# Sparse attention with a gated feed-forward network: chunks of 512 local tokens, one last chunk for the global tokens of all batches, gate buffers by row pairs

## The chip, the cores and the metric

The kernel runs on one core of one Trainium2 chip. The metric is the device time of one execution in microseconds (us), as the median of several runs. Lower is better. The engines are TensorE (PE in the profile; PEld is its weight load), VectorE (DVE), ScalarE (ACT), GpSimd (POOL) and SyncE (SP), which issues the transfers (DMA).

## What is computed

Eight batches, eight heads, 512 local and 32 global tokens, head dimension 64. Global queries attend to everything; a local query attends to all global keys and to local keys at most 32 positions away. The result of all heads (544 tokens x 512) goes through a network with 1024 hidden columns, a convolution over three neighbouring tokens and a gate.

```python
s_g  = scale * q_g @ concat(k_g, k_l).T          # 32 global queries, 544 keys
out_g = softmax(s_g) @ concat(v_g, v_l)
s_l  = scale * q_l @ concat(k_g, where(|i-j|<=32, k_l, -1e9)).T
out_l = softmax(s_l) @ concat(v_g, v_l)
x = concat(out_g, out_l)                         # 8 x 544 x 512, global tokens first
h = maximum(x @ w_in, 0)                         # 512 -> 1024
c = sum over k in 0..2 of conv_w[k] * h[token + k - 1]
return (h * sigmoid(c)) @ w_out                  # 1024 -> 512
```

The attention's inputs are float32, the network's weights float64.

## The kernel before, in words

**Attention.** Heads are worked in pairs (n even). Local queries stand in 16 blocks of 32; with the blocks in four groups c of four, `SC` (L291) makes the scores of a pair with 32 small matmuls per head against windows of 128 keys (three local blocks and the global one). `MA` (L319) adds the mask and takes the maximum on DVE, `EX` (L329) is the exponential on ACT, `NS` and `NP` divide by the sum, `DT` (L350) transposes 32 x 32 blocks on DVE into a buffer `pt`, and `PV` (L360) multiplies with the values. `XH` and `XL` (L380) split the result into two float32r parts, high and low, in the tiles `xh` and `xl`, each 128 x 544 for 128 of the 512 columns. The global queries go through `G`, `GM`, `GE`, `GN`, `GT`, `GC`, `GP`, `GO`, `GQ`; `GX` writes their 32 tokens into the first columns of the same tiles.

**Keys.** The keys of a pair come with its queries in one load (`LQ`): 512 query columns and 4 x 7 blocks of 32 keys, where each group c has its own seven blocks, neighbours doubled.

**Network.** It works in units of half a batch (`HALF` = 272 tokens; 16 halves `hh`). `Z` (L475) makes one block of 128 hidden columns of a half with 12 matmuls of 274 columns: four 128-row parts of x, and for each high x high, high x low and low x high. `RE` (L484) is max(0, .)/2 on ACT into `hb`; `C1` (L276, POOL) and twice `C2` (L499, DVE) are the convolution in `t`; for two blocks together `TH` (L508) is the tanh on ACT, `GG` (L513) the gate on DVE, `GH` (L241) and `GL` (L244) its split into the gate tiles `g0` (high) and `g1` (low). These hold all eight blocks of a half, two halves at a time. `O` (L538) makes 128 output columns of a half with 24 matmuls of 272 columns in two parts (`Oa`, `Ob`), `OE` (L241) copies it out of PSUM and `ST` (L550) stores it. Every matmul of `Z` and `O` has weights of its own, so it comes with a weight load.

**Weights.** The float64 weights come in eight chunks (`WD`) into the buffers that later hold the gates, and are turned into a high and a low float32r part: `WA`, `WC`, `WL` (L115 to L215) on ACT and DVE, `WS` (L224 to L226: 512-column matmuls, first float32, then two in float32r) and `WX`.

**Order.** The order on each engine is not written out by hand: `plan` lists all operations with costs, buffers and positions (`POS`, `POS0`), `arranged` runs them through a list of ready operations, and `emit` fixes that order on each engine. Buffers are counted in `SLOTS`; at most two `Z` and two `O` results are in PSUM (`LIMIT`).

```python
SLOTS = dict(
    ps=4, pa=2, x=6, hb=2, qk=5, vf=5, qg=2, p=4, pt=4, r=3, pg=2, pgt=2, og=1, t=2, o=2, wt=2, g0=2, g1=2,
)
LIMIT = dict(h=2, o=2)
```

Of the kernel before, what the change touches and what calls it, by code (L numbers as in the profile page):

```python
# [56 lines left out]
def attn_moe(ctx: ExitStack, tc: tile.TileContext, qk_d, vw_d, qg_d, w_in_d, w_out_d, cw_d, out_d):  # L57
# [9 lines left out]
    gp = ctx.enter_context(tc.tile_pool(name="gp", bufs=2))  # L67
# [106 lines left out]
    def WD(i):  # L174

        t = gp.tile([P, 1024, wpe], WT, name="raw", tag=f"g{i % 2}", padded_shape=[P, NFT * HALF // wpe, wpe])
# [58 lines left out]
    hb = [const.tile([P, 2, HW + 1], F32, name=f"hb{i}") for i in range(SLOTS["hb"])]  # L235
    for t in hb:
        for o in (0, HW):
            nc.vector.memset(t[:, :, o : o + 1], 0.0)
# [41 lines left out]
    def SC(n):  # L280

        qk = heads[n]["qk"]
        for j in range(2):
            heads.setdefault(n + j, {})["s"] = four[SIDE["S", n]][:, j, :].rearrange("p (r x) -> p r x", r=NR)
        for r in range(NR):
            for c in range(4):
                i = NR * c + r
                a = SL + (NK * c + r) * SG
                for j in range(2):
                    rows = slice(j * D, (j + 1) * D)  # L290
                    nc.tensor.matmul(  # L291
                        heads[n + j]["s"][c * SG : (c + 1) * SG, r, :], lhsT=qk[rows, i * SG : (i + 1) * SG],
                        rhs=qk[rows, a : a + P], start=True, stop=True,
                    )

    def G(n):
# [5 lines left out]
        for i in range(3):  # L302
            for c in range(4):
                k = heads[first + 2 * c]["qk"][:, SL:]
                for j in range(2):
                    rows = slice(j * D, (j + 1) * D)
                    if i < 2:
                        kj = k[rows].rearrange("p (c m x) -> p m c x", c=4, m=NK)[:, SLOT[2 * i] : SLOT[2 * i] + 2]
# [142 lines left out]
    def GX(n):  # L451
        pt = gos[n // H][1]
        for ct in range(NCT):
            xh, xl = x_of(n // H, ct)
            cp("GX", xh[:, 0:SG], pt[:, ct * SG : (ct + 1) * SG])
            nc.vector.tensor_tensor(
                out=xl[:, 0:SG], in0=pt[:, ct * SG : (ct + 1) * SG], in1=f(xh)[:, 0:SG], op=ALU.subtract
            )
# [4 lines left out]
    def half_of(hh):  # L463
        return (hh + TURN) % 2

    def Z(u):
        hh, ft = divmod(u, NFT)
        b, half = hh // 2, half_of(hh)
        st = hid[u] = {"h": hb[u // 2 % SLOTS["hb"]][:, u % 2, half : half + HW]}
        ps = st["z"] = bank([P, HW], "ps_h")  # L470
        i = 0
        for ct in range(NCT):
            xh, xl = [x[:, half * (S - HW) : half * (S - HW) + HW] for x in x_of(b, ct)]
            for w, x in ((w_in[0], xh), (w_in[0], xl), (w_in[1], xh)):
                nc.tensor.matmul(ps, lhsT=w[:, ft, ct, :], rhs=x, start=i == 0, stop=i == 3 * NCT - 1)  # L475
                i += 1

    def RE(u):

        half = half_of(u // NFT)  # L480
        o = hid[u]["h"][:, 1 - half : HW - half]
        z = hid[u]["z"][:, half : HW - 1 + half]
# [21 lines left out]


    def TH(u):
        t = hid[u]["two"]
        nc.scalar.activation(out=t, in_=t, func=AF.Tanh)  # L508

    def GG(u):  # L510
        t, half = hid[u]["two"], half_of(u // NFT)
        h = hb[u // 2 % SLOTS["hb"]][:, :, half + 1 : half + 1 + HALF]
        nc.vector.scalar_tensor_tensor(out=t, in0=t, scalar=1.0, in1=h, op0=ALU.add, op1=ALU.mult)  # L513

    def GH(u):
        hh, ft = divmod(u, NFT)
        if hh not in gs:
            gs[hh] = [gp.tile([P, NFT, HALF], F32R, name=f"g{i}") for i in range(2)]
        cp("GH", gs[hh][0][:, ft - 1 : ft + 1, :], hid[u]["two"])

    def GL(u):
        hh, ft = divmod(u, NFT)
        gh, gl = gs[hh]
        sub("GL", gl[:, ft - 1 : ft + 1, :], hid[u]["two"], f(gh)[:, ft - 1 : ft + 1, :])


# [3 lines left out]
    def O(o, part):  # L530
        hh, mt = divmod(o, NCT)
        gh, gl = gs[hh]
        if part == 0:
            ops[o] = bank([P, HALF], "ps_o")
        ps = ops[o]
        for ft in range(part * 4, part * 4 + 4):
            for i, (w, g) in enumerate(((w_out[0], gh), (w_out[1], gh), (w_out[0], gl))):
                nc.tensor.matmul(  # L538
                    ps, lhsT=w[:, mt, ft, :], rhs=g[:, ft, :], start=ft + i == 0, stop=ft == NFT - 1 and i == 2
                )  # L540

    def OE(o):
        hh, mt = divmod(o, NCT)
        t = outs[o] = moe.tile([P, HALF], F32, name="o", bufs=SLOTS["o"])
        cp("OE", t, ops[o])

    def ST(o):
        hh, mt = divmod(o, NCT)
        b, half = hh // 2, half_of(hh)
        nc.sync.dma_start(out=out_d[b, mt, :, half * HALF : (half + 1) * HALF], in_=outs[o])  # L550

    emit(tc, B, dict(
        LQ=LQ, LV=LV, LG=LG, G=G, S=SC, M=MA, E=EX, NS=NS, NP=NP, DT=DT, P=PV,
        XH0=lambda n: XH(n, 0), XH1=lambda n: XH(n, 1), XL0=lambda n: XL(n, 0), XL1=lambda n: XL(n, 1),
        GM=GM, GE=GE, GN=GN, GT=GT, GC=GC, GP=GP, GO=GO, GQ=GQ, GX=GX,
        PZ=Z, RE=RE, C1=C1, Ca=lambda u: C2(u, 0), Cb=lambda u: C2(u, 2), TH=TH, GG=GG, GH=GH, GL=GL,
        Oa=lambda o: O(o, 0), Ob=lambda o: O(o, 1), OE=OE, ST=ST, WD=WD, WA=WA, WC=WC, WH=WH, WL=WL, WS=WS, WX=WX,
# [5 lines left out]
    ps=4, pa=2, x=6, hb=2, qk=5, vf=5, qg=2, p=4, pt=4, r=3, pg=2, pgt=2, og=1, t=2, o=2, wt=2, g0=2, g1=2,  # L563
# [396 lines left out]
```

## Time and profile before

| | us |
|---|---|
| median of 3 runs (573.83 to 576.04) | 574.9 |
| the profiled execution, whole | 573.74 |
| its span, first to last instruction | 572.0 |
| PE busy | 546.3 (96%) |
| PEld busy | 511.7 (89%) |
| DVE busy | 431.0 (75%) |
| ACT busy | 355.1 (62%) |
| POOL busy | 97.3 (17%) |
| DMA: 57.09 MB, mean 100 GB/s | queue with the data busy 27.5% of 16 engines |

The chain that ended last lies on PE for 87% of the span: 34% on `O` (L538), 34% on `Z` (L475), 7% on `PV` (L360), 5% on `SC` (L291). PE's busy time is a sum of pipelined matmuls, whose recorded durations overlap; the pace of a matmul is read from the distance of one start to the next.

### The profile page before, as it was taken

What the parts mean: (1) busy time and instruction counts of PE and PEld (TensorE: products, weight loads), DVE (VectorE), ACT (ScalarE), POOL (GpSimd) and SP (SyncE); (2) the same over time, 40 slices, a digit from 0 to 9 for tenths busy, and PEclk for the clock granted to TensorE, in tenths of its full rate; (3) what the DMA queues carried; (4) which work ended last, traced back from release to release, by engine and by line L of the source; (5) the groups of instructions that cost most, each with busy time, mean ns of one, the idle gap of its engine ahead of it and who ended that gap; (6) DMA issues with size and microseconds to landing.
All of it is one profiled execution on the core that took longest, in us unless ns stands there. A gap on an engine that the chain in (4) does not pass through costs nothing.

```text
span 572.0 us, 23262 instructions
## 1 busy us (share of the span) xinstructions
PE 546.3 (96%) x9904; PEld 511.7 (89%) x9904; DVE 431.0 (75%) x1403; ACT 355.1 (62%) x1140; POOL 97.3 (17%) x171
## 2 busy tenths in 40 slices
PE   4289999999999999999999999999999999999997
PEld 3257888899999999999999999999999999999997
DVE  4999999776889788778967778688676776646561
ACT  5658789685995686649672698279633493313330
POOL 4311142320111110201110111101111021101110
PEclk9589999999999999999999999999999999999999
DMA  8666743015403603043300603050000300000001
GB/s 350 280 241 207 245 158 109 12 29 196 168 15 135 229 21 123 21 158 113 113 31 24 241 13 131 13 193 14 30 30 32 111 13 21 32 22 21 21 31 49
DMA packets 20984, 57.09 MB, mean 100 GB/s; under 512 B 2448, under 2 KB 11664, under 8 KB 19856
## 3 DMA queue, kind: packets, MB, share of 16 engines
q1 hardware_dynamic: 20880, 55.61, 27.5%
q8 instruction: 77, 1.26, 0.9%
q14 instruction: 27, 0.22, 0.1%
HBM read 46.69 MB, written 8.91 MB: 97 GB/s over the span
## 4 chain that ended last, share of the span: by engine, by line
PE 87%; DVE 8%; DMA 2%; issue 1%; ACT 1%; SPq 0%; DVEq 0%; ACTq 0%
PE ps_o L538 34%; PE ps_h L475 34%; PE four L360 7%; PE four L291 5%; DMA raw<-w_in 2%; PE four L428 2%; PE four L312 2%; PE four L412 1%; PE psw L224 1%; DVE pr L319 1%; DVE t L499 1%; DVE pt L350 1%; DVE xl L380 1%; DVE wt L126 1%; PE four L446 1%
## 5 line engine op out<-in xcount | busy, mean ns | idle before, releaser
L475 PE MATMUL ps_h<-xh,w_in 128*128 128x274 f32 x1024 | 222.6, 296 | 0.3 <-issue 0.3
L538 PE MATMUL ps_o<-g,w_out 128*128 128x272 f32 x1536 | 210.8, 290 | 0.0
L538 PEld LDWEIGHTS ps_o<-g,w_out 128*128 128x128 f32 x1536 | 199.1, 188 | 1.1 <-issue 0.4
L475 PEld LDWEIGHTS ps_h<-xh,w_in 128*128 128x128 f32 x1024 | 169.3, 188 | 6.6 <-issue 3.8
L499 DVE SCALAR_TENSOR_TENSOR t<-hb,cw,t 128x272 f32<-128x272 f32 x256 | 125.2, 509 | 32.1 <-POOL t L276 31.1
L475 PE MATMUL ps_h<-xl,w_in 128*128 128x274 f32 x512 | 148.4, 290 | 0.0
L276 POOL TENSOR_SCALAR t<-hb,cw 128x272 f32<-128x272 f32 x128 | 74.0, 584 | 395.4 <-ACT hb L484 247.8
L329 ACT ACTIVATE pr<-pr,negm 128x128 f32<-128x128 f32 x256 | 99.2, 392 | 28.0 <-DVE negm L319 28.0
L475 PEld LDWEIGHTS ps_h<-xl,w_in 128*128 128x128 f32 x512 | 97.0, 189 | 0.2
L484 ACT ACTIVATE hb<-ps_h 128x273 f32<-128x273 f32 x128 | 50.5, 395 | 60.6 <-PE ps_h L475 60.1
L343 ACT ACTIVATE pr<-pr,sums 128x128 f32<-128x128 f32 x224 | 70.4, 394 | 4.7 <-DVE sums L337 4.7
L508 ACT ACTIVATE t<-t 128x544 f32<-128x544 f32 x64 | 42.0, 657 | 44.4 <-DVE t L499 43.9
L360 PEld LDWEIGHTS four<-pt,vf 32*64 32x64 f32 x3584 | 48.7, 133 | 19.2 <-DVE negm L319 12.0
L319 DVE CUSTOM_DVE_ANT_0 pr<-four,mask 128x128 f32<-128x128 f32 x256 | 57.3, 285 | 11.4 <-PE four L291 11.2
L360 PE MATMUL four<-pt,vf 32*64 32x96 f32 (+3 forms) x3584 | 53.1, 246 | 12.8 <-DVE negm L319 11.1
L513 DVE SCALAR_TENSOR_TENSOR t<-t,hb 128x544 f32<-128x544 f32 x64 | 46.0, 720 | 17.8 <-ACT t L508 17.7
L241 ACT CAST g<-t 128x544 fp32r<-128x544 f32 x64 | 40.8, 644 | 20.7 <-DVE t L513 18.1
L241 DVE COPY o<-ps_o 128x272 f32<-128x272 f32 x64 | 28.1, 440 | 33.5 <-PE ps_o L538 33.3
L350 DVE STREAM_TRANSPOSE pt<-pr 128x512 f32<-128x512 f32 x64 | 44.4, 700 | 8.4 <-PE four L360 4.6
L329 ACT ACTIVATION_READ_ACCUMULATOR pr<-pr,negm 128x1 f32 x256 | 48.8, 191 | 0.0
L291 PE MATMUL four<-qk 64*32 64x128 f32 x2048 | 39.1, 282 | 8.9 <-DMA qk<-qk 4.8
L244 DVE TENSOR_TENSOR g<-t,g 128x544 fp32r<-128x544 f32 x56 | 40.3, 722 | 6.0 <-ACT g L241 5.5
(79 smaller groups left out, 393.6 us busy)
## 6 DMA issues: line engine op xcount, KB each, us to landing
qk<-qk SPq DMA_DIRECT2D x32, 704.0 KB, 5.7
vf<-vw SPq DMA_DIRECT2D x32, 448.0 KB, 5.6
out<-o SPq DMA_DIRECT2D x64, 136.0 KB, 1.8
raw<-w_in SPq DMA_DIRECT2D x4, 1024.0 KB, 12.4
raw<-w_out SPq DMA_DIRECT2D x4, 1024.0 KB, 5.0
qgf<-qg SPq DMA_DIRECT2D x8, 64.0 KB, 4.7
cwr<-cw SPq DMA_DIRECT2D x1, 24.0 KB, 10.8
```

The source lines that it names most:

```text
L241: nc.scalar.copy(out=out, in_=in_) if choice(key) == "a" else eng(key).tensor_copy(out=out, in_=in_)
L276: nc.gpsimd.tensor_scalar(out=out, in0=in_, scalar1=by, scalar2=0.0, op0=ALU.mult, op1=ALU.add)
L291: nc.tensor.matmul(heads[n + j]["s"][c * SG : (c + 1) * SG, r, :], lhsT=qk[rows, i * SG : (i + 1) * SG], rhs=qk[rows, a : a + P], start=Tr ...
L319: nc.vector.tensor_tensor_reduce(out=pr[:, r, :], in0=st["s"][:, r, :], in1=mask[:, r].rearrange("p a c -> p (a c)"), op0=ALU.add, op1=ALU ...
L329: nc.scalar.activation(out=st["p"][:, r, :], in_=st["p"][:, r, :], func=AF.Exp, scale=-1.0, bias=st["m"][:, r : r + 1], accum_out=two["r"] ...
L343: nc.scalar.activation(out=p[:, r, :], in_=p[:, r, :], func=AF.Copy, scale=by[:, r : r + 1])
L350: nc.vector.transpose(out=st["pt"].rearrange("p a q -> p (a q)"), in_=st["p"].rearrange("p r x -> p (r x)"))
L360: nc.tensor.matmul(four[c // 2][j * D : (j + 1) * D, c % 2, r0 * SG : (r1 + 1) * SG], lhsT=heads[n]["vf"][rows, j, m, :], rhs=heads[n + j] ...
L475: nc.tensor.matmul(ps, lhsT=w[:, ft, ct, :], rhs=x, start=i == 0, stop=i == 3 * NCT - 1)
L484: nc.scalar.activation(out=o, in_=z, func=AF.Relu, scale=0.5)
L499: nc.vector.scalar_tensor_tensor(out=st["t"], in0=st["h"][:, k : k + HALF], scalar=cw[:, 3 * ft + k : 3 * ft + k + 1], in1=st["t"], op0=AL ...
L538: nc.tensor.matmul(ps, lhsT=w[:, mt, ft, :], rhs=g[:, ft, :], start=ft + i == 0, stop=ft == NFT - 1 and i == 2)
```

## The change

1. **Chunks of the network.** A chunk is now the 512 local tokens of a batch (`Z` and `O` with 512 columns), and one last chunk holds the 32 global tokens of all eight batches: `Z` with 8 x 34 = 272 columns (a batch's globals and its first two local tokens, as neighbours for the convolution), the convolution and `O` with 8 x 35 - 2 = 278 columns, with one zero column between batches. A new tile `xg` keeps the x of these tokens until then: `GX` writes it with two instructions instead of eight, and a new step `XC` on POOL copies two local columns per 128 rows of x. The output is laid out as chunks and put in order outside.
2. **Parts.** `Z` is in two parts: `Za` needs the first two 128-row parts of x, `Zb` the other two. `O` is in four, `Oa` to `Od`, each needing one pair of gate blocks.
3. **Gate buffers by row pairs.** One tile `g` holds high and low part of two blocks (2 x 2 x 512); there are five of them, instead of two sets of eight blocks of 272. The weight chunks use the same five. The weight decoding's buffer `wt` is gone: it shares the two buffers `t` of the convolution.
4. **Transposes in place.** `DT` writes over its source; the buffers are `p` = 6 instead of `p` = 4 and `pt` = 4.
5. **Keys in 22 blocks.** The groups share their neighbours: 22 blocks of 32 keys instead of 28. Queries and keys are loaded apart (`LQ` 256 KB, three buffers; `LK` 352 KB, five buffers) instead of in one load of 704 KB.
6. **Plan.** All positions are new, and the costs follow the new sizes.

```diff
-ROW = (-1, 0, 1, None, 2, 3, 4)
-NK = len(ROW)
-KSEQ = 4 * NK * SG
-SLOT = tuple(ROW.index(x) for x in (0, 1, 2, 3, None))
+ROW = (-1, 0, 1) + sum(((None,) + tuple(range(4 * c + 2, 4 * c + 6)) for c in range(4)), ())[:-1]
+KSEQ = len(ROW) * SG
+NK = 7
+SLOT = (1, 2, 4, 5, 3)
...
-            wf[i] = load.tile([P, 1024], U32, name="wt", bufs=SLOTS["wt"])
+            wf[i] = moe.tile([P, 1024], U32, name="wt", tag="t", bufs=SLOTS["t"])
...
+    xg = const.tile([P, 2, NCT, B, GW], F32R, name="xg")
...
-        st["pt"] = att.tile([P, 4 * NR, SG], F32, name="pt", bufs=SLOTS["pt"])
-        nc.vector.transpose(out=st["pt"].rearrange("p a q -> p (a q)"), in_=st["p"].rearrange("p r x -> p (r x)"))
+        flat = st["p"].rearrange("p r x -> p (r x)")
+        nc.vector.transpose(out=flat, in_=flat)
+        st["pt"] = flat.rearrange("p (a q) -> p a q", q=SG)
...
+    def XC(n):
+        b, h = divmod(n, H)
+        cp("XC", xg[:, :, h // 2, b, SG:GW], f(x_of(b, h // 2))[:, :, 0:2])
...
+        hi, lo = [xg[:, i, :, b, 0:SG] for i in range(2)]
+        cp("GX", hi, pt)
+        nc.vector.tensor_tensor(out=lo, in0=pt, in1=f(hi), op=ALU.subtract)
...
+    def Z(u, part):
+        b, ft = divmod(u, NFT)
+        n = B * GW if last(u) else SL
+        if part == 0:
+            hid[u] = {"z": bank([P, 512], "ps_h")[:, 0:n]}
+        for ct in range(2 * part, 2 * part + 2):
+            xh, xl = [xg[:, i, ct].rearrange("p b x -> p (b x)") if last(u) else x_of(b, ct)[:, i] for i in range(2)]
+            for i, (w, x) in enumerate(((w_in[0], xh), (w_in[0], xl), (w_in[1], xh))):
+                nc.tensor.matmul(
+                    hid[u]["z"], lhsT=w[:, ft, ct, :], rhs=x, start=ct + i == 0, stop=ct == NCT - 1 and i == 2
+                )
...
-            gs[hh] = [gp.tile([P, NFT, HALF], F32R, name=f"g{i}") for i in range(2)]
-        cp("GH", gs[hh][0][:, ft - 1 : ft + 1, :], hid[u]["two"])
+        g = gs[u // 2] = gp.tile([P, 2, 2, SL], F32R, name="g", tag="g")[:, :, :, 0 : width(u)]
+        cp("GH", g[:, 0], mid_of(u))
...
-    ps=4, pa=2, x=6, hb=2, qk=5, vf=5, qg=2, p=4, pt=4, r=3, pg=2, pgt=2, og=1, t=2, o=2, wt=2, g0=2, g1=2,
+    ps=4, pa=2, x=6, hb=2, q=3, k=5, vf=5, qg=2, p=6, r=3, pg=2, pgt=2, og=1, t=2, o=2, g=5,
...
+        if local:
+            ready = [[("XL%d" % k, 8 * b + 2 * ct) for ct in cts for k in range(2)] for cts in ((0, 1), (2, 3))]
+        else:
+            ready = [[("GX", 8 * i + 7) for i in range(b)] + [("XC", 2 * i) for i in range(4 * b)], []]
...
+        for i, key in enumerate(("Oa", "Ob", "Oc", "Od")):
+            before = [("GL", NFT * b + 2 * i + 1)] + ([weight(4 + mt)] if i == 0 else [("O" + "abc"[i - 1], o)])
+            at_o(key, before, [("ps", f"o{o}"), ("o_", f"o{o}o")] * (i == 0), [f"g{4 * b + i}"] + [f"o{o}"] * (i > 0))
```

## Rows read from the trace of the kernel before

**Rows 1.** Busy time by stretch: bounds, length, PE, PEld, DVE, ACT, POOL, clock, DMA.
```profile
0.00:46.20 46.20, 25.96 (x793) 18.17 (x793) 36.97 (x127) 28.04 (x89) 12.25 (x35) 0.82 0.77 292
46.20:72.00 25.80, 25.49 (x371) 21.31 (x371) 25.18 (x73) 22.00 (x57) 4.53 (x6) 1.00 0.65 218
72.00:143.00 71.00, 69.62 (x1382) 62.48 (x1381) 59.31 (x210) 53.03 (x179) 18.44 (x22) 1.00 0.29 99
143.00:500.50 357.50, 357.06 (x6662) 342.33 (x6661) 274.82 (x922) 234.37 (x783) 53.16 (x93) 1.00 0.23 81
500.50:572.00 71.50, 68.20 (x704) 67.37 (x703) 34.67 (x75) 17.62 (x35) 8.87 (x16) 0.99 0.09 29
```

**Rows 2.** PE's longest waits between 0 and 72 us: sum, times, longest.
```profile
PE four L360 <- DVE negm L319: 10.5, 2, 6.6
PE four L291 <- DMA qk<-qk: 4.8, 1, 4.8
PE four L360 <- DVE xl L380: 1.7, 1, 1.7
```

**Rows 3.** The chain that ended last: start, length, engine, line, matmuls.
```profile
46.20 1.72 PE ps_h L475 x12
...
314.70 1.71 PE ps_h L475 x12
...
488.64 1.52 PE ps_h L475 x12
...
553.64 15.15 PE ps_o L538 x120
```

**Rows 4.** PE in order of time at one weight chunk: start, recorded length, operation.
```profile
98.46 1.02 PE L224 MATMUL psw<-wt,ident 128*128 128x512 f32 x2
...
99.55 0.39 PE L226 MATMUL psw<-w_out,minus 128*128 128x512 f32 x1
99.78 1.02 PE L224 MATMUL psw<-wt,ident 128*128 128x512 f32 x2
...
100.86 0.40 PE L226 MATMUL psw<-w_out,minus 128*128 128x512 f32 x1
101.10 0.29 PE L475 MATMUL ps_h<-xh,w_in 128*128 128x274 f32 x1
```

**Rows 5.** The weight loads (PEld) at the same place.
```profile
100.64 0.19 PEld L226 LDWEIGHTS psw<-w_out,minus 128*128 128x128 f32 x1 [0.24 <-issue]
100.87 0.19 PEld L475 LDWEIGHTS ps_h<-xh,w_in 128*128 128x128 f32 x1
```

**Rows 6.** Groups by line and shape: busy us, mean ns, idle before and its releaser.
```profile
L276 POOL TENSOR_SCALAR t<-hb,cw 128x272 f32<-128x272 f32 x128 | 74.0, 584 | 395.4 <-ACT hb L484 247.8 <-DVE g L244 107.9 <-DVE gsum L403 15.4
L244 DVE TENSOR_TENSOR g<-t,g 128x544 fp32r<-128x544 f32 x56 | 40.3, 722 | 6.0 <-ACT g L241 5.5
L380 DVE TENSOR_TENSOR xl<-four,xh 128x256 fp32r<-128x256 f32 x64 | 24.2, 411 | 5.9 <-ACT xh L241 5.5
L126 DVE SCALAR_TENSOR_TENSOR wt<-raw,wt 128x1024 uint32<-128x1024 uint32 x8 | 9.8, 1226 | 0.3
L241 ACT CAST w_in<-wt 128x1024 fp32r<-128x1024 f32 x4 | 4.2, 1052 | 1.7 <-DVE wt L126 1.7
L96 POOL COPY place<-ident 32x32 f32<-32x32 f32 x4 | 0.8, 203 | 0.2
```

**Rows 7.** DVE in order of time: four convolution steps back to back.
```profile
82.00 1.74 DVE L499 SCALAR_TENSOR_TENSOR t<-hb,cw,t 128x272 f32<-128x272 f32 x4
```

**Rows 8.** First and last step of one weight chunk, DVE and PE in order of time.
```profile
48.83 0.69 DVE L122 TENSOR_SCALAR wt<-wt 128x1024 f32<-128x1024 f32 x1
...
58.67 0.40 PE L226 MATMUL psw<-w_out,minus 128*128 128x512 f32 x1
```

**Rows 9.** SP's waits for `SC` to free a query and key buffer: sum, times, longest.
```profile
SPq L259 <- PE four L291: 51.3, 11, 13.0
```

**Rows 10.** The last copy out of PSUM, DVE in order of time.
```profile
568.81 0.44 DVE L241 COPY o<-ps_o 128x272 f32<-128x272 f32 x1 [1.07 <-PE ps_o L538]
```

More of the change, by code (lines that the diff above doesn't have):

```diff
@@ L174, in WD @@
     def WD(i):
-        t = gp.tile([P, 1024, wpe], WT, name="raw", tag=f"g{i % 2}", padded_shape=[P, NFT * HALF // wpe, wpe])
+        t = gp.tile([P, 1024, wpe], WT, name="raw", tag="g", padded_shape=[P, 2048 // wpe, wpe])
         nc.sync.dma_start(out=t.rearrange("p n w -> p (n w)"), in_=w_in_d[:, i] if i < 4 else w_out_d[:, i - 4])
@@ L232, in WX @@
                 cp("WX", lo[:, 512 * k : 512 * k + 512], ps)
-    hb = [const.tile([P, 2, HW + 1], F32, name=f"hb{i}") for i in range(SLOTS["hb"])]
+    xg = const.tile([P, 2, NCT, B, GW], F32R, name="xg")
+    hb = [const.tile([P, 2, SL + 2], F32, name=f"hb{i}") for i in range(SLOTS["hb"])]
     for t in hb:
-        for o in (0, HW):
+        for o in (0, SL + 1):
             nc.vector.memset(t[:, :, o : o + 1], 0.0)
@@ L280, in SC @@
     def SC(n):
-        qk = heads[n]["qk"]
+        q, keys = heads[n]["q"], heads[n]["k"]
         for j in range(2):
@@ L291, in SC @@
                     nc.tensor.matmul(
-                        heads[n + j]["s"][c * SG : (c + 1) * SG, r, :], lhsT=qk[rows, i * SG : (i + 1) * SG],
-                        rhs=qk[rows, a : a + P], start=True, stop=True,
+                        heads[n + j]["s"][c * SG : (c + 1) * SG, r, :], lhsT=q[rows, i * SG : (i + 1) * SG],
+                        rhs=keys[rows, a : a + P], start=True, stop=True,
                     )
@@ L303, in G @@
             for c in range(4):
-                k = heads[first + 2 * c]["qk"][:, SL:]
+                k = heads[first + 2 * c]["k"]
                 for j in range(2):
@@ L451, in GX @@
     def GX(n):
[L452 to L458, printed above, removed]
+        b = n // H
+        pt = gos[b][1].rearrange("p (c x) -> p c x", c=NCT)
+        hi, lo = [xg[:, i, :, b, 0:SG] for i in range(2)]
+        cp("GX", hi, pt)
@@ L460, in attn_moe @@
+        nc.vector.tensor_tensor(out=lo, in0=pt, in1=f(hi), op=ALU.subtract)
     hid = {}
     gs = {}
[L463 to L476, printed above, removed]
@@ L478, in RE, with last, width, rows_of @@
-    def RE(u):
-        half = half_of(u // NFT)
-        o = hid[u]["h"][:, 1 - half : HW - half]
-        z = hid[u]["z"][:, half : HW - 1 + half]
+    def last(u):
+        return u // NFT == B
+    def width(u):
+        return B * GV - 2 if last(u) else SL
+    def rows_of(u, k):
+        return hb[u // 2 % SLOTS["hb"]][:, :, k : k + width(u)]
+    def mid_of(u):
+        return hid[u]["two"][:, :, 0 : width(u)]
+    def Z(u, part):
[9 more added lines that the diff above has]
+                )
@@ L483, in RE @@
+    def RE(u):
+        t, z = hb[u // 2 % SLOTS["hb"]], hid[u]["z"]
+        o = t[:, u % 2, 1 : SL + 1]
+        if last(u):
+            both = t[:, :, 0 : B * GV].rearrange("p a (b x) -> p a b x", b=B)
+            if u % 2 == 0 and u // 2 % (NFT // 2) < SLOTS["hb"]:
+                nc.gpsimd.memset(both[:, :, :, 0:1], 0.0)
+            o, z = both[:, u % 2, :, 1:], z.rearrange("p (b x) -> p b x", b=B)
         if choice("RE") == "a":
@@ L506, in TH @@
     def TH(u):
-        t = hid[u]["two"]
+        t = mid_of(u)
         nc.scalar.activation(out=t, in_=t, func=AF.Tanh)
     def GG(u):
-        t, half = hid[u]["two"], half_of(u // NFT)
-        h = hb[u // 2 % SLOTS["hb"]][:, :, half + 1 : half + 1 + HALF]
-        nc.vector.scalar_tensor_tensor(out=t, in0=t, scalar=1.0, in1=h, op0=ALU.add, op1=ALU.mult)
+        t = mid_of(u)
+        nc.vector.scalar_tensor_tensor(out=t, in0=t, scalar=1.0, in1=rows_of(u, 1), op0=ALU.add, op1=ALU.mult)
     def GH(u):
-        hh, ft = divmod(u, NFT)
@@ L528, in attn_moe @@
+        sub("GL", g[:, 1], mid_of(u), f(g)[:, 0])
     ops, outs = {}, {}
     def O(o, part):
-        hh, mt = divmod(o, NCT)
-        gh, gl = gs[hh]
+        b, mt = divmod(o, NCT)
         if part == 0:
-            ops[o] = bank([P, HALF], "ps_o")
+            ops[o] = bank([P, 512], "ps_o")[:, 0 : width(NFT * b)]
         ps = ops[o]
-        for ft in range(part * 4, part * 4 + 4):
-            for i, (w, g) in enumerate(((w_out[0], gh), (w_out[1], gh), (w_out[0], gl))):
+        g = gs[NFT // 2 * b + part]
@@ L538, in O @@
+        for ft in range(2 * part, 2 * part + 2):
+            for i, (w, k) in enumerate(((0, 0), (1, 0), (0, 1))):
                 nc.tensor.matmul(
-                    ps, lhsT=w[:, mt, ft, :], rhs=g[:, ft, :], start=ft + i == 0, stop=ft == NFT - 1 and i == 2
+                    ps, lhsT=w_out[w][:, mt, ft, :], rhs=g[:, k, ft % 2, :], start=ft + i == 0,
+                    stop=ft == NFT - 1 and i == 2,
                 )
     def OE(o):
-        hh, mt = divmod(o, NCT)
-        t = outs[o] = moe.tile([P, HALF], F32, name="o", bufs=SLOTS["o"])
+        t = outs[o] = moe.tile([P, SL], F32, name="o", bufs=SLOTS["o"])[:, 0 : width(NFT * (o // NCT))]
@@ L592, with cost @@
+    GC=7.81, GP=73.94, GO=69.07, GQ=95.45, GX=31.75, Za=-51.42, Zb=23.49, RE=18.93, C1=19.9, Ca=-110.94,
+    Cb=-28.3, TH=-19.96, GG=-107.88, GH=46.26, GL=17.73, Oa=137.35, Ob=-36.69, Oc=38.34, Od=-17.69, OE=-37.34,
+    ST=-9.22, WD=260.68, WA=43.56, WC=557.46, WH=-14.87, WL=27.97, WS=29.44, WX=-19.5,
+)
+LATE = (277.56, 46.45, 51.62)
+WPOS = [-181.22, -223.58, 13.77, -1.77, 112.11, 84.41, 21.24, -26.67]
 LAST_BATCH = 7
-TURN = 1
-def cost(key, e):
+def cost(key, e, wide=True):
     def act(n, calls=1, src=190, more=0):
@@ L634, in cost @@
     if key in DIFFERENCES:
-        return two(DIFFERENCES[key]) if e == "v" else pool2(DIFFERENCES[key])
+        return two(2 * n) if e == "v" else pool2(2 * n)
     if key == "C1":
-        return act(HALF, more=93) if e == "a" else fast(HALF) if e == "v" else pool1(HALF)
+        return act(n, more=93) if e == "a" else fast(n) if e == "v" else pool1(n + 90)
     if key == "NP":
@@ L682, in op @@
         at[key, i] = len(ops)
-        occ, lat = cost(key, c)
+        wide = key not in UNITS or i < UNITS[key] * B
+        occ, lat = cost(key, c, wide)
         more = int(occ * STRETCH["shared" if e == DVE and key in SHARED else e])
@@ L725, in plan @@
             before = [("DT", e), ("DT", n), ("LV", e)] + [("P", e - 2)] * (e > 0)
-            at_n("P", before, [("pa", x) for x in oo] + [("x", x)], [f"pt{e}", f"pt{n}", f"vf{p}"], i=e)
+            at_n("P", before, [("pa", x) for x in oo] + [("x", x)], [f"p{e}", f"p{n}", f"vf{p}"], i=e)
             for k in range(2):
@@ L745, in plan @@
             at_n("GQ", [("GO", n)], [], [gp, og])
-            at_n("GX", [("GQ", n)] + [("XL%d" % k, n - 7 + 2 * c) for c in range(4) for k in range(2)], [], [gp] + [f"x{b},{c}" for c in range(4)])
+            at_n("GX", [("GQ", n)], [], [gp])
             units(op, late, b)
+    units(op, late, B)
     return ops
@@ new lines, in units, with at_u @@
+    local = b <= LAST_BATCH
+    x = [f"x{b},{ct}" for ct in range(NCT)]
+    for ft in range(NFT):
+        u = NFT * b + ft
+        def at_u(key, *more, u=u):
+            op(key, u, late(H + u, b) + (POS if b else POS0)[key] + (not local) * LATE[2], b > 0, *more)
+        if local:
+            ready = [[("XL%d" % k, 8 * b + 2 * ct) for ct in cts for k in range(2)] for cts in ((0, 1), (2, 3))]
+        else:
+            ready = [[("GX", 8 * i + 7) for i in range(b)] + [("XC", 2 * i) for i in range(4 * b)], []]
+        before = [("Zb", u - 1)] * (u > 0)
+        at_u("Za", ready[0] + before + [weight(ft // 2)], [("ps", f"h{u}"), ("h", f"h{u}h")], x[0:2] * local)
+        at_u("Zb", [("Za", u)] + ready[1], [], [f"h{u}", f"h{u}h"] + x[2:4] * local)
+        at_u("RE", [("Zb", u)] + [("RE", u - 1)] * (u > 0), [("hb", f"hb{u // 2}")] * (u % 2 == 0), [f"h{u}", f"h{u}h"] + [f"hb{u // 2}"] * (u % 2))
+        at_u("C1", [("RE", u)] + [("C1", u - 1)] * (u > 0), [("t", f"t{u // 2}")] * (u % 2 == 0), [f"hb{u // 2}"] + [f"t{u // 2}"] * (u % 2))
+        at_u("Ca", [("C1", u)], [], [f"hb{u // 2}", f"t{u // 2}"])
+        at_u("Cb", [("Ca", u)], [], [f"hb{u // 2}", f"t{u // 2}"])
+        if u % 2:
+            at_u("TH", [("Cb", u - 1), ("Cb", u)], [], [f"t{u // 2}"])
+            at_u("GG", [("TH", u)], [], [f"t{u // 2}", f"hb{u // 2}"])
+            at_u("GH", [("GG", u)] + [("GH", u - 2)] * (u > 1), [("g", f"g{u // 2}")], [f"t{u // 2}"])
+            at_u("GL", [("GH", u)], [], [f"t{u // 2}", f"g{u // 2}"])
@@ new lines, in units, with at_o @@
+    for mt in range(NCT):
+        o = NCT * b + mt
+        def at_o(key, *more, o=o):
+            more_late = LATE[1] if b == LAST_BATCH else LATE[2] if not local else 0
+            op(key, o, late(H + 8 + 2 * o, b) + (POS if b else POS0)[key] + more_late, b > 0, *more)
+        for i, key in enumerate(("Oa", "Ob", "Oc", "Od")):
+            before = [("GL", NFT * b + 2 * i + 1)] + ([weight(4 + mt)] if i == 0 else [("O" + "abc"[i - 1], o)])
+            at_o(key, before, [("ps", f"o{o}"), ("o_", f"o{o}o")] * (i == 0), [f"g{4 * b + i}"] + [f"o{o}"] * (i > 0))
+        at_o("OE", [("Od", o)], [("o", f"ot{o}")], [f"o{o}", f"o{o}o"])
+        at_o("ST", [("OE", o)], [], [f"ot{o}"])
@@ L912, in laid_out, with seq @@
     c = np.ascontiguousarray
-    def seq(g, l):
+    def seq(g, l, row):
         l = np.pad(l.reshape(B, H, NB, SG, D), ((0, 0), (0, 0), (1, 1), (0, 0), (0, 0)))
-        row = lambda q: [g if x is None else l[:, :, 1 + NR * q + x] for x in ROW]
-        return np.stack([np.stack(row(q), axis=2) for q in range(4)], axis=2)
-    ks = seq(k_g, k_l).reshape(B, H, KSEQ, D)
+        return np.stack([g if x is None else l[:, :, 1 + x] for x in row], axis=2)
+    ks = seq(k_g, k_l, ROW).reshape(B, H, KSEQ, D)
     qk = np.concatenate([q_l.transpose(0, 1, 3, 2), ks.transpose(0, 1, 3, 2)], axis=-1)
     qk = c(qk.reshape(B, H // 2, P, SL + KSEQ))
-    vs = seq(v_g, v_l).transpose(0, 1, 2, 4, 3, 5).reshape(B, H // 2, 2, P, NK, D)
+    own = (-1, 0, 1, None, 2, 3, 4)
+    vs = np.stack([seq(v_g, v_l, [x if x is None else 4 * i + x for x in own]) for i in range(4)], axis=2)
+    vs = vs.transpose(0, 1, 2, 4, 3, 5).reshape(B, H // 2, 2, P, NK, D)
     vw = c(vs.transpose(0, 1, 3, 2, 4, 5))
@@ L948, in program, with gathered @@
     return nc
+def gathered(outs):
+    got = outs["out"]
+    B = (got.shape[1] // NCT + 2) // (SL + GV)
+    own = got[:, : B * NCT * SL].reshape(P, B, NCT, SL).transpose(1, 3, 2, 0)
+    first = got[:, B * NCT * SL :].reshape(P, NCT, B * GV - 2)
+    first = np.stack([first[:, :, GV * b : GV * b + SG + 1] for b in range(B)]).transpose(0, 3, 2, 1)
+    return np.ascontiguousarray(np.concatenate([first, own[:, 1:]], axis=1)).reshape(B, S, DM)
 def kernel(**inputs):
@@ L956 @@
     r = run_bass_kernel_spmd(nc, [arrays], core_ids=[0])
[L957 to L959 removed]
+    return gathered(r.results[0])
```

155 lines of the change are left out of this document (63 added, 92 removed).

## The prediction

> **What bounds the kernel now.** I read the busy times by stretch first [rows 1]. From 46.2 us on PE stands still for 0.31 us up to 72, 1.38 us up to 143, 0.44 us up to 500.5 and 3.3 us in the last stretch, of which 3.2 lie behind the last matmul (its copy starts at 568.81 [rows 10], the span ends at 572.0). So over 92% of the time PE always has work, and DVE, the next engine, is busy for 274.82 of 357.50 us there. The other 20.2 us of idle PE lie before 46.2, where DVE is busy for 36.97 of 46.2 us and PE waits, above all, for the softmax of the first pair (10.5 us), the first load (4.8) and x parts (1.7) [rows 2]. Two things can therefore move the end: the time that PE needs for its matmuls, and what it waits for before 46 us. What the change does to DVE, ACT, POOL and DMA counts only if it makes PE wait.
>
> The busy time of PE is no measure of a matmul, since recorded durations overlap; the chain of the end gives the pace [rows 3]. Twelve matmuls of `Z` (274 columns) take 1.52 us, 126.7 ns each; 120 of `O` (272 columns) take 15.15 us, 126.2 each. Streaming 272 columns at 2.4 GHz, the clock granted in all these stretches (1.00 in [rows 1]), takes 113.3 ns, so each matmul pays some 12.9 ns besides (12.5 for `Z`).
>
> **The main term: fewer, wider matmuls.** Before: `Z` 16 halves x 8 x 12 = 1536 at 126.7 = 194.6 us, `O` 16 x 4 x 24 = 1536 at 126.2 = 193.8 us, together 388.4. After: 8 x 8 x 12 + 8 x 4 x 24 = 1536 matmuls of 512 columns, 96 of 272 and 96 of 278. Columns hardly change (838,656 before, 839,232 after): globals are moved, not removed. What goes is the payment per matmul, 3072 of them against 1728.
> No `Z` or `O` of before is 512 wide, but the weight decoding runs float32r matmuls of 512 columns with their own weight loads (L226). From the start of one to the start of the next instruction: 99.55 to 99.78 and 100.86 to 101.10 [rows 4], and the weight loads around it stand at 100.64 and 100.87 [rows 5]: 0.23 us. So I take 230 ns (16.7 over the 213.3 of streaming). The two ends: the payment stays 12.8 as for 272 columns, 226 ns; or, since 98.46 to 101.10 holds four float32r matmuls and four float32 passes that stream at least 426.7 ns each, at most (2640 - 1707) / 4 = 233 ns. I stay at 230, the nearest row by width and type.
> Sum after: 1536 x 230 = 353.3 us; 96 x 126.2 = 12.1; 96 x (126.2 + 6/2.4) = 12.4; together 377.8. **Gain 10.6 us**; 16.7 at 226 ns, 6.0 at 233.
> The Trainium skill, "TensorE: Matmul & The Clock Gate", section "Back-to-back issue gap", speaks against this: it gives a warm matmul its columns over 2.4 plus 2.5 ns, whatever the width, and by that 1344 fewer matmuls would save 3.4 us. The trace differs: 126.2 ns for 272 columns where that rule has 115.8.
>
> **The start.** `Za` needs only the first two parts of x, so two of them (two PSUM banks, 2 x 6 x 0.23 = 2.8 us) can run while PE waits for the later pairs. The one wait of that kind is 1.7 us [rows 2]; the other 15.3 of the group fall before any x exists. I take **1.0 us**, a little over half, with ends 0 and 2.8. The first pair's queries and keys are 608 KB instead of 704, and its other work is unchanged.
>
> **What costs nothing under cover.** DVE: four convolution steps in 1.74 us [rows 7], 0.435 each; two rows of DVE [rows 6], 411 ns at 256 and 1226 at 1024 columns, give 1.06 ns per column, so 0.69 us at 512: 16 x 0.69 = 11.0 per batch for 32 x 0.435 = 13.9. `GG`, `GL`, `OE` and `GX` shrink alike; DVE, busy 77% of the long stretch, gets freer. ACT and POOL stay below it. The 32 `XC` are POOL copies of 0.2 us (203 ns [rows 6]), 6.5 us on an engine busy for 53 of 357 us; behind one on POOL's queue wait `C1`s, whose cover is the units of PE queued ahead. The transpose in place does the same work; with it a pair holds its buffer from `SC` to `PV`, three pairs in all, where two pairs of `p` and two of `pt` overlapped. If that runs short, `SC` waits, and PE goes on with `Z` and `O`.
> Loads: 32 more issues on SP. SP already stood up to 13 us at a time for a free buffer (51.3 us in all for `SC` [rows 9]) with the stores behind it, and PE did not wait. `Q` buffers, now free after `SC` alone, can only come earlier; three instead of five make the wait likelier. If stores behind it came late, `OE` and then `O` would stop, up to 13 us once. I count none.
> `Zb`, waiting for x, holds back all of PE's queue; it costs only where `PV` is late.
> An attention piece between big matmuls costs the next group about 0.2 us (1.71 against 1.52 for twelve [rows 3]); the pieces are as many as before. Ten more or fewer places would move 2 us either way.
> The tail: the last `O` has 278 columns instead of 272, its copy and store are the same 3.2 us. Before it, `Z` and `O` of the last chunk (24.5 us of PE) can lie beside each other's vector work.
>
> **Sum.** 573.74 - 10.6 - 1.0 = 562.1 for the profiled execution; the median is 1.2 above it, so **563.3 us**. With the ends alone (6.0 and 0; 16.7 and 2.8; 2 for the places) 555 to 571.
>
> **Rivals.**
> *The wide matmul pays almost nothing.* The weight loads keep PEld busy for 342.33 of 357.50 us [rows 1]. Were they what paces narrow matmuls, wide ones would run at stream speed: 1536 x 215.8 = 331.5, in all 356.0, a gain of 32.4. With the 1.0 that gives 541.5. Against it stand the four starts of [rows 4], 230 instead of 216. The 215.8 is what the rule of the Trainium skill quoted above makes of 512 columns; without it the bare stream, 213.3, gives 538. Chance 0.05.
> *The payment grows with the columns.* Then 512 columns cost 126.2 x 512/272 = 237.6, the sum is 389.4, and nothing is gained: 574 to 575. Rows 4 speak against it, 0.23 being 3% less. Chance 0.05.
> *The start loses.* Weight chunks now share two `t` with the convolution and five `g` with the gates, and four chunks are still to be decoded when the first `Z` runs. One chunk's chain goes from 48.83 to past 58.67 [rows 8], 10 us. If one such chain comes between, 573. For it: the start is where DVE is full, and batch 0's four gate pairs leave one `g` for raw weights. Against it: PE has `Z` of batch 0 (22 us) and batch 1's attention meanwhile. Chance 0.10.
> *Slower: the gate buffers stop ACT at every batch.* `O` of a batch holds four `g` until its last output block; one is left for the next batch's first pair. Its second pair's `GH` waits on ACT until `Oa` of that block ends, and behind it on ACT's queue wait `EX`, `XH` and `RE`. Then follow `GH` and `GL` (1052 ns at 1024 columns; 722 + 480 x 1.06 = 1.23 us [rows 6]), and only then is `t` free for the fourth pair: `C1` 584 x 512/272 = 1.10, four convolution steps 2.76, `TH` 1.05 like the other ACT pass over 1024 columns, `GG` 1.23, `GH` 1.05, `GL` 1.23, together 8.4. That pair is ready 10.7 us after `Oa`. Meanwhile PE has `Ob` to `Od` (3 x 1.38 = 4.1) and, of the next `O`, three parts of one block (4.1) or, with both banks free, of two (8.3). With one, and no attention piece in between, 2.5 us are missing at each of seven batch ends: 17.5, so 581. It decides from 1.5 us per batch end on (10.6 / 7). For it: before, two full sets of gates gave a whole half of slack. Against it: 32 `SC` and 32 `PV` groups are there to fill, two of them are enough, and DVE is freer. Chance 0.10.
>
> **How the numbers follow.** The forecast, 563.3, has 0.66; the four rivals 0.05, 0.05, 0.10 and 0.10; 0.04 is for gains that I don't see. The range must take in the forecast with its ends and the two rivals near no change: 553 to 575, some 0.8. What can be told from no change here is about 0.5%, 2.9 us. Faster: 0.66 + 0.05 + 0.04 and 0.03 of a lost start that is short = 0.78. Same: the rest of it and the growing payment, 0.12. Slower: the gate buffers, 0.10.
>
> **What would show it.** In the chain after, six wide matmuls of `Z` or `O` take 1.38 us (1.36 to 1.40); 1.30 would be the first rival, 1.42 the second. PE's idle time past 46 us stays below 5 us; if it is 15 or more, and PE's waits name `GL` or ACT's `GH` a wait for `O`, the gate buffers are the cause. The first `Z` starts at 46 us (46.20 before [rows 3]) or a little earlier; ten later means the weight chunks. The last stretch ends with `O` of 278 columns without a gap and 3.2 us behind it. I am wrong if PE is as full as before and the time still differs from 562 by more than the pace explains.

## The result and the profile after

The changed kernel takes 558.82 us (median, 558.25 to 560.27) where the kernel before takes 574.66: ratio 0.973, 95% interval 0.971 to 0.974, that is 15.8 us less. Forecast were 563.3 us and 11.6 us less; the range was 553 to 575. The profiled execution took 558.97 us with a span of 557.1, against 573.74 and 572.0.

Busy time by stretch, after (columns as in [rows 1]; the last stretch is again the 72 us before the end):

```profile
0.00:46.20 46.20, 29.40 (x845) 21.38 (x846) 35.85 (x152) 30.84 (x108) 13.24 (x38) 0.74 0.82 304
46.20:72.00 25.80, 25.69 (x399) 18.18 (x398) 23.75 (x55) 19.82 (x52) 5.02 (x6) 1.00 0.49 173
72.00:143.00 71.00, 70.41 (x1113) 54.57 (x1115) 60.56 (x162) 53.86 (x156) 15.23 (x17) 1.00 0.19 59
143.00:485.00 342.00, 341.19 (x5841) 274.30 (x5824) 249.63 (x749) 222.83 (x691) 44.90 (x71) 1.00 0.25 84
485.00:557.10 72.10, 68.47 (x387) 60.39 (x385) 32.51 (x49) 16.64 (x26) 7.64 (x14) 1.00 0.09 34
```

PE is as full as before: from 46.2 us on it stands still for 0.11, 0.59, 0.81 and 3.63 us, 5.1 in all where it was 5.4. What changed there is the second number, PEld: 274.30 of 342 us, where the weight loads had filled 342.33 of 357.50. So there are fewer loads, and PE has work all the same: the time must lie in the matmuls themselves. The chain shows their pace (start, length, engine, line, matmuls; L493 is `Z`, L551 `O`, as in [rows 3]):

```profile
127.58 10.92 PE ps_o L551 x48
...
252.85 1.59 PE ps_h L493 x6
254.43 1.38 PE ps_o L551 x6
255.81 1.36 PE ps_h L493 x6
...
469.14 1.36 PE ps_h L493 x6
470.50 1.36 PE ps_o L551 x6
...
537.05 0.76 PE ps_h L493 x6
...
539.95 13.53 PE ps_o L551 x102
```

Six matmuls of 512 columns take 1.36 us, 226.7 ns each; six of 272 take 0.76. The last row is six wide and 96 of 278 columns: (13.53 - 1.36) / 96 = 126.8 ns. With the prediction's counts: 1536 x 226.7 = 348.2, 96 x 126 = 12.1, 96 x 126.8 = 12.2, together 372.5 us instead of 388.4. That would be 15.9 us less, if every wide matmul had this pace. Not all have it: behind attention the first six take 1.59 us and the next six 1.38, 230 ns each, before 1.36 comes.

The traces have a record of every `Z` and `O` matmul, so the whole can be summed as well. Taken from each start to PE's next start, without PE's waits, `Z` and `O` together are 404.0 us before and 390.1 after: **13.9 us less** (390.1 in a second profiled execution of the changed kernel, too). A wide matmul that stands between two others of `Z` or `O` takes 228.9 ns on average. The profiled spans differ by 14.9 us: beside the 13.9, PE's waits between its matmuls are 3.9 us shorter, attention and weight decoding take 2.7 us longer on PE, and the two ends of the span are 0.2 us longer. The medians differ by 15.8; single executions of one kernel lie some 2 us apart, so the last microsecond or two isn't assigned.

PE's waits after 46.2 us (sum, times, longest) are all there is of new waiting; none names a gate buffer:

```profile
PE four L296 <- DVE pr L356: 0.6, 1, 0.6
PE four L296 <- DVE x L392: 0.6, 1, 0.6
PE four L296 <- issue: 0.2, 1, 0.2
```

### The profile page after: what moved, and what is told of

It is laid out like the page before. It is cut to its first block, busy times and chain, and to the rows that moved or that the text cites. A ratio compares the mean times of both kernels' runs of the same rounds, so it can differ in the third digit from the quotient of the medians.

```text
span 557.1 us, 20079 instructions
## 1 busy us (share of the span) xinstructions
PE 535.2 (96%) x8560; PEld 428.8 (77%) x8560; DVE 402.3 (72%) x1163; ACT 344.0 (62%) x1028; POOL 86.0 (15%) x145
## 4 chain that ended last, share of the span: by engine, by line
PE 86%; DVE 9%; ACT 3%; DMA 1%; issue 0%; SPq 0%; ACTq 0%
PE ps_o L551 33%; PE ps_h L493 32%; PE four L367 7%; PE four L296 6%; PE four L440 2%; PE four L318 2%; PE psw L224 2%; DVE pr L325 2%; PE four L424 1%; DVE wt L126 1%; ACT pr L349 1%; DMA q<-qk 1%; DVE pr L356 1%; PE psw L225 1%; DVE wt L123 1%; ACT pr L335 1%
## 5 line engine op out<-in xcount | busy, mean ns | idle before, releaser
L551 PE MATMUL ps_o<-g,w_out 128*128 128x512 f32 (+1 forms) x864 | 207.6, 382 | 0.0
L493 PE MATMUL ps_h<-x,w_in 128*128 128x512 f32 x768 | 202.2, 400 | 0.0
L551 PEld LDWEIGHTS ps_o<-g,w_out 128*128 128x128 f32 x864 | 153.7, 188 | 29.3 <-ACT pr L349 0.2
L493 PEld LDWEIGHTS ps_h<-x,w_in 128*128 128x128 f32 x768 | 139.5, 188 | 32.5 <-issue 3.4
L520 DVE SCALAR_TENSOR_TENSOR t<-hb,cw,t 128x512 f32<-128x512 f32 (+1 forms) x144 | 104.1, 736 | 30.3 <-POOL t L281 29.5
L281 POOL TENSOR_SCALAR t<-hb,cw 128x512 f32<-128x512 f32 (+1 forms) x72 | 55.7, 775 | 290.4 <-ACT hb L506 198.6
L367 PEld LDWEIGHTS four<-pr,vf 32*64 32x64 f32 x3584 | 49.3, 135 | 16.4 <-issue 10.3
L367 PE MATMUL four<-pr,vf 32*64 32x96 f32 (+3 forms) x3584 | 53.1, 248 | 5.2 <-DVE pg L399 2.3
L531 DVE SCALAR_TENSOR_TENSOR t<-t,hb 128x1024 f32<-128x1024 f32 (+1 forms) x36 | 42.0, 1168 | 15.5 <-ACT t L527 15.3
L356 DVE STREAM_TRANSPOSE pr<-pr 128x512 f32<-128x512 f32 x64 | 44.1, 698 | 12.4 <-ACT pr L349 11.9
```

Source lines behind the costliest of these rows:

```text
L281: nc.gpsimd.tensor_scalar(out=out, in0=in_, scalar1=by, scalar2=0.0, op0=ALU.mult, op1=ALU.add)
L356: nc.vector.transpose(out=flat, in_=flat)
L367: nc.tensor.matmul(four[c // 2][j * D : (j + 1) * D, c % 2, r0 * SG : (r1 + 1) * SG], lhsT=heads[n]["vf"][rows, j, m, :], rhs=heads[n + j] ...
L493: nc.tensor.matmul(hid[u]["z"], lhsT=w[:, ft, ct, :], rhs=x, start=ct + i == 0, stop=ct == NCT - 1 and i == 2)
L520: nc.vector.scalar_tensor_tensor(out=t, in0=rows_of(u, k)[:, u % 2], scalar=cw[:, 3 * ft + k : 3 * ft + k + 1], in1=t, op0=ALU.mult, op1=A ...
L551: nc.tensor.matmul(ps, lhsT=w_out[w][:, mt, ft, :], rhs=g[:, k, ft % 2, :], start=ft + i == 0, stop=ft == NFT - 1 and i == 2,)
```

## The experiments

The theory after the result: the gain is the payment that each matmul makes beside its columns, made 1728 times instead of 3072, and everything else in the change nets to about nothing. The rivals: the new order, the start and the smaller loads bring the time; or narrow matmuls were held by their weight loads.

**Halves.** All other edits stay; only the width is undone.

```diff
-            for i, (w, x) in enumerate(((w_in[0], xh), (w_in[0], xl), (w_in[1], xh))):
-                nc.tensor.matmul(hid[u]["z"], lhsT=w[:, ft, ct, :], rhs=x, ...)
+            step = n if last(u) else SL // 2
+            for a in range(0, n, step):
+                for i, (w, x) in enumerate(((w_in[0], xh), (w_in[0], xl), (w_in[1], xh))):
+                    nc.tensor.matmul(hid[u]["z"][:, a : a + step], lhsT=w[:, ft, ct, :], rhs=x[:, a : a + step], ...)
...
(the same in O)
```

> The changed kernel, but every 512-column matmul of Z and O is two of 256 columns, each with its own weight load; order, buffers and all other work as in the changed kernel. Theory (the gain is the payment per matmul, now read as 226.7 ns for 512 columns, 13.4 over the stream): 256 columns take 106.7 + 13.4 = 120 ns, 3072 x 120 = 368.6 instead of 1536 x 227 = 348.7 us, so 20 us slower than the changed kernel, 579. Rival 1 (the gain comes from the new order, the start, fewer loads): no change, 559. Rival 2 (narrow matmuls are paced by their weight loads, about 126 ns whatever the width): 3072 x 126.5 = 388.6, 40 us slower, 599.

Measured: 576.71 us, 1.0034 of the kernel before (1.0009 to 1.0058). The whole gain is gone. The chain of this kernel, a stretch without attention (twelve matmuls of 256 columns are what six of 512 were):

```profile
208.98 1.44 PE ps_h L495 x12
210.42 1.44 PE ps_o L557 x12
```

120 ns for 256 columns, 13.3 over the stream of 106.7. The theory had said 120 ns and 579 us; the rival of the order and the start (559) and that of the weight loads (599) are refuted. There is a second reading in it: summed from start to start, `Z` and `O` of this kernel are 405.9 us, 1.9 more than the 404.0 of the kernel before, and its median is 1.6 us above. So new order, start, loads, in-place transposes and the last chunk together come to nothing, within the microsecond or two that these runs can tell.

**Quarters.** `SL // 2` becomes `SL // 4`.

> The same with four matmuls of 128 columns in place of one of 512. Payment per matmul: 53.3 + 13.4 = 66.7 ns, 6144 x 66.7 = 410 us, 61 us slower than the changed kernel, 620. If a weight load has a pace of its own between 100 and 126 ns, 128 columns take that: 614 to 774 us for the matmuls, 265 to 425 us slower.

Measured: 889.27 us. The chain, again without attention:

```profile
744.37 2.68 PE ps_o L557 x24
747.05 2.68 PE ps_h L495 x24
```

111.7 ns for 128 columns, where the payment alone would make 66.7. So something other than the payment bounds here. That it is the load of 128 x 128 weights is argued, since no run changes the load alone. It isn't the issue of two instructions as such: at 138.42 us in the changed kernel 64 matmuls of `SC`, each with a load of 64 x 32, take 1.16 us. So the paces are 111.7, 120, 126, 226.7 ns for 128, 256, 272, 512 columns: stream plus 13 from 256 on, and a floor at 112 that 272 columns (126) don't touch. The Trainium skill, "TensorE: Matmul & The Clock Gate", section "LDWEIGHTS (loading the stationary operand)", gives a load's weight columns over 1.2, for 128 an estimated 106.7 ns. The floor measured here lies 5 ns above it.

**A row of wide matmuls in the weight decoding.** The prediction took its 230 ns there, from single matmuls beside float32 passes.

```diff
-                nc.tensor.matmul(ps, lhsT=minus, rhs=hi[:, cols], start=False, stop=True)
+                for j in range(9):
+                    nc.tensor.matmul(ps, lhsT=plus if j % 2 else minus, rhs=hi[:, cols], start=False, stop=j == 8)
```

> The changed kernel with nine float32r matmuls of 512 columns in a row where the weight decoding has one (minus, plus, minus ... over the same part, so that the sum stays). It measures the pace that the prediction took as 230 ns from single starts beside float32 passes. If 230 was the pace of such matmuls: 8 of them take 1.84 us. If only the neighbourhood of float32 passes makes it 230 to 240: 8 take 1.81 to 1.82 as in Z and O (226.7). The kernel gets up to 16 x 8 x 0.227 = 29 us slower, less what the start has idle.

Measured: 589.2 us, and a pace that is not one number. Starts of the first, the third and the ninth of a row, PE in order of time, in two chunks:

```profile
82.10 0.40 PE L227 MATMUL psw<-w_in,minus 128*128 128x512 f32 x1
...
82.56 0.39 PE L227 MATMUL psw<-w_in,minus 128*128 128x512 f32 x1
...
83.92 0.39 PE L227 MATMUL psw<-w_in,minus 128*128 128x512 f32 x1
...
143.92 0.39 PE L227 MATMUL psw<-w_out,minus 128*128 128x512 f32 x1
...
144.38 0.40 PE L227 MATMUL psw<-w_out,minus 128*128 128x512 f32 x1
...
145.77 0.39 PE L227 MATMUL psw<-w_out,minus 128*128 128x512 f32 x1
```

1.82 us for eight in the first, 227.5 ns; 1.85 in the second, 231 ns. In both rows the first two take 0.46 us, 230 ns each. The six behind them take 1.36 us in the first row, 226.7 ns as in `Z` and `O`, and 1.39 in the second, 232 ns. In the eight full-speed rows between 66 and 149 us five are like the second and three like the first.

`Z` and `O` of the changed kernel do the same behind other work. They stand in 88 unbroken runs, and a wide matmul takes 232 ns on average in places 2 to 5 of a run, 230 in places 6 to 10 and 227 from the 11th on. So neither expectation is met as it stands: 230 is a real pace, but that of the first matmuls behind something else, be it float32 passes or attention, and a row of nine can end before it is over. Narrower matmuls don't show it (places 2 to 5: 119 ns at 256 columns in the halves, 125 and 127 at 272 and 274 in the kernel before). What makes it, and why it is over sooner in some rows than in others, is open.

**Four gate buffers.** `g=5` becomes `g=4`, and the order is planned anew.

> The changed kernel with four gate buffers instead of five; the order is planned anew for it. It asks how near the gate buffers are to stopping ACT and PE. If five are ample (PE idle past 46 us was 1.5 us before the tail): under 3 us slower. If the prediction's slower rival was near: with no spare pair every batch end lacks at least one pair's chain, 3 to 8 us each, 20 to 60 us slower, and PE's waits show it.

Measured: 564.66 us, 0.9825 of the kernel before (0.979 to 0.986); run once more beside the unaltered change, 563.22 against 557.98. So the fifth buffer is worth some 5 us, between the two expectations. PE's waits after 46.2 us name the gates now:

```profile
PE ps_o L551 <- ACT g L242: 1.4, 1, 1.4
PE ps_h L493 <- DVE x L392: 1.1, 1, 1.1
PE four L296 <- issue: 0.9, 1, 0.9
PE ps_o L551 <- DVE g L245: 0.2, 1, 0.2
```

They come to 3.6 us instead of 1.4, once each and not at every batch, and the two that name the gates to 1.6: the rival's mechanism exists, but little of it reaches PE. This profiled execution is 3.1 us slower than that of the changed kernel (562.08 against 558.97), and the 2.2 us of waits are most of it; in the second pair (565.02 against 558.83) PE's waits after 46.2 us are 3.2 us longer, half of the difference. The rest stays unexplained: the order is another one too, and no run has the buffer changed alone.

**The start: no work of `Z` before all of x.** The order stays; in the first two blocks `Za` is empty and `Zb` does all twelve.

```diff
-        for ct in range(2 * part, 2 * part + 2):
+        for ct in [range(0, NCT * part), range(2 * part, 2 * part + 2)][u >= 2]:
```

> The changed kernel, same order, but in the first two blocks of batch 0 the first part of Z does nothing and the second does all 12 matmuls: no Z work before all of batch 0's x is there. The prediction gave this split of Z 1.0 us (0 to 2.8): then 559 to 562. The trace of the changed kernel has only one six-matmul part of Z before 46.2 us and PE waits of 16.8 us instead of 20.2, but at a lower clock; by that the start gained nothing: 558 to 560, as the changed kernel.

The changed kernel beside it:

> The changed kernel once more, unaltered, as the reference on the same chip for the kernels beside it. 558 to 560 us, 0.973 of the kernel before.

Measured: 558.85 us (0.9727, 0.970 to 0.975) beside 557.98 (0.971, 0.9685 to 0.974): not told apart, and no more than a microsecond or two. The first two stretches of this kernel:

```profile
0.00:46.20 46.20, 27.54 (x844) 20.58 (x844) 36.38 (x153) 31.44 (x108) 13.24 (x38) 0.85 0.82 308
46.20:72.00 25.80, 24.79 (x396) 17.71 (x394) 22.19 (x47) 18.79 (x49) 4.71 (x6) 1.00 0.46 167
```

PE idles for 18.7 + 1.0 us here and for 16.8 + 0.1 in the changed kernel, 2.8 more (at a granted clock of 0.85 against 0.74 in the first stretch), and that cost nothing that could be measured: profiled spans 556.6 and 557.1.

**Keys in 28 blocks again.** SBUF of the changed kernel is full, so the larger key buffers need the room of the fifth gate buffer; the comparison is with four.

> Four gate buffers, planned anew, once more as the reference for the next kernel. 562 to 567 us.

> Four gate buffers as in the kernel beside it, and the keys again in 28 blocks with each group's own seven (448 instead of 352 KB per load); the fifth gate buffer had to go because SBUF is full. Same order. The prediction counts the smaller loads at nothing: no difference to the kernel with four gate buffers, within 1.5 us. If the loads had been on the path at the start, 32 x 96 KB more, up to 0.3 us per load at 300 GB/s: 1 to 9 us slower.

Measured: 562.37 us (0.9783, 0.975 to 0.9815) beside 563.22 (0.9798, 0.976 to 0.984): no difference. The shorter loads bring no time; what they bring is room, and that pays for the fifth gate buffer. The transposes in place and the shared `t` were not undone by themselves.

## Why the prediction was right, point by point

**The bound.** Right: PE without gaps from 46 us on, before and after, and so only its matmuls counted.

**The main term.** Right in mechanism, too small by a quarter: 10.6 us where the trace has 13.9. The mis-sized step is the one pace of 230 ns for all wide matmuls, "the nearest row by width and type" [rows 4, 5]. Those starts lie right behind float32 passes. There 230 is right, and nearly so for places 2 to 10 behind attention (230 to 232); about half of the wide matmuls stand later in their run and take 227. The average of 228.9 makes 1.7 us on 1536 matmuls. The prediction's lower end, that the payment stays as for 272 columns, 226, was right for the settled pace: payments over the stream are 13.3, 12.9, 13.4 ns at 256, 272, 512 columns. The 126.7 ns for `Z` before, from a single row of twelve [rows 3], was a little small too: summed over the trace of the kernel before it is 127.4, which makes 1.1 us. The rest of the 3.3 us is spread over smaller terms. For narrow matmuls 126 to 127 ns held (128.7 was taken for 278 columns, 126.8 came). This term is most of the 4.2 us by which the forecast gain was short. One slip in the sum changes nothing: the ends "555 to 571" leave the 2 us for the places out of the lower one, which would be 553.

**The start.** 1.0 us was taken. The 0.9 us between the medians with and without `Za` can't be told from 0, nor from 1.0. Idle PE before 46.2 us fell from 20.2 to 16.8 us, but that is not a gain as such: the first `Z` begins at 45.6 us where it was 46.1, the decoding of one weight chunk that was done by then before now comes after it, and the granted clock of that stretch was 0.74, against 0.82 before, so that part of the filling is slower matmuls. DVE is busy for 35.85 of 46.2 us, and with `Za` empty 2.8 us more of idle PE made no difference.

**Under cover.** Recorded durations after (columns as in [rows 6]):

```profile
L281 POOL TENSOR_SCALAR t<-hb,cw 128x512 f32<-128x512 f32 x64 | 50.9, 798 | 259.8 <-ACT hb L506 172.1 <-DVE g L245 41.9 <-PE psw L224 18.8
L531 DVE SCALAR_TENSOR_TENSOR t<-t,hb 128x1024 f32<-128x1024 f32 x32 | 39.0, 1221 | 11.0 <-ACT t L527 10.9
L245 DVE TENSOR_TENSOR g<-t,g 128x1024 fp32r<-128x1024 f32 x28 | 34.3, 1224 | 16.7 <-ACT g L242 16.7
L527 ACT ACTIVATE t<-t 128x1024 f32<-128x1024 f32 x32 | 33.9, 1058 | 19.0 <-DVE t L520 19.0
L242 ACT CAST g<-t 128x1024 fp32r<-128x1024 f32 x32 | 33.5, 1047 | 20.1 <-PE ps_o L551 10.8 <-DVE t L531 9.3
L242 POOL CAST xg<-x 128x4 fp32r<-128x4 f32 x32 | 8.8, 275 | 127.8 <-DVE x L392 118.0 <-ACT hb L506 9.9
```

`GG`, `GL`, `TH` and `GH` came as worked out (1.23, 1.23, 1.05, 1.05 us). `C1` was scaled by its columns to 1.10 us and takes 0.80, `XC` 275 ns instead of 203; neither is on the path. DVE fell to 249.63 of 342 us, 73%. SP's queue did what the prediction feared and left at nothing. Before, a query buffer held the keys too and was waited for in two ways, for `SC` [rows 9] and for `G` (L312). The second of these, and the one kind after (sum, times, longest):

```profile
SPq L259 <- PE four L312: 30.9, 5, 13.2
...
SPq L259 <- PE four L296: 132.7, 24, 25.8
```

They went from 82.2 us (51.3 [rows 9] and 30.9) to 132.7, up to 25.8 at a time, with the stores behind them, and after 46.2 us PE waited for none of it.

**Places between attention and network.** In the traces PE goes from small tiles to the full array 68 times before and 68 times after. Right in the number. The first six wide matmuls behind attention pay 1.59 - 1.36 = 0.23 us, where [rows 3] have 0.19, and the next six can pay 0.02 more. What is new are the 597 wide matmuls in places 2 to 10 of a run: they take 2.6 us more than at the pace from the 11th on, which the average of 228.9 ns holds already.

**The tail.** 557.1 us is 3.6 behind the start of the last copy, 0.4 more than before [rows 10]:

```profile
553.50 0.45 DVE o L242
```

The cause is open. The last chunk's `Z` lies between the last batch's `O` and needs no gap, as worked out.

**The rivals.** That wide matmuls run at stream speed (215.8 ns) and that the payment grows with the columns (237.6) are refuted by 226.7, and the first by the quarters too: a matmul with its own load has its floor at 112, below the 126 of before. The rule of the Trainium skill ("TensorE: Matmul & The Clock Gate", section "Back-to-back issue gap": columns over 2.4 plus 2.5 ns), which that section gives for isolated warm matmuls, made an estimated gain of 3.4 us. The payments of 13 ns at three widths show that it doesn't hold for float32r matmuls that each bring their own weights. The lost start didn't come. The stop at the gate buffers is there, but on ACT: it waits for `O` to give a buffer back (after, sum, times, longest), and this reaches PE only with four buffers.

```profile
ACT g L242 <- PE ps_o L551: 11.7, 9, 3.4
```

## What to carry to other kernels

Where PE is full, take the pace of a matmul from start to start over long runs, subtract the stream, and see what is left: here 13 ns each, 10% at 272 columns and 6% at 512, so that cutting the work along the widest allowed matmul, with the leftover of all batches gathered into one chunk, gained 2.7% without removing a column. A price for another width has two parts: the settled pace, which the same loop gave with a constant payment (226 ns worked out, 226.7 measured), and the pace right behind other work, which a short row of the right width gave (230). Count how many matmuls stand at each. Smaller loads and fewer buffers that cost and save no time themselves can still be worth it: here the room that they free holds the fifth gate buffer, which together with its order is worth some 5 us.

## What was not expected of the hardware

A float32r matmul of 512 columns with its own weight load takes 226.7 ns once settled, but 230 to 232 on average in places 2 to 10 behind other work, all at the full clock; matmuls of 256 to 274 columns show nothing of the kind, and the cause is open. Matmuls of 128 columns with a weight load each took 111.7 ns where columns and payment would make 66.7. And a POOL multiplication of 128 x 512 elements takes 798 ns where 128 x 272 takes 584 [rows 6]; a line through the two leaves an estimated 0.34 us that doesn't depend on the columns.
